# Sparse attention and two expert layers on one core: probabilities transposed as two 64-row halves, and a new order of the vector and scalar work around them

## The chip, the core and the metric

The kernel runs on one core of one Trainium2 chip. The metric is the device time of one execution in microseconds (us): the median of three timed runs. One further execution was recorded by the hardware profiler, and every trace row below is of that one. Engine names are those of the profile: PE (matmul) and PEld (the loads of its stationary operand), DVE (vector), ACT (scalar), POOL (GpSimd), SP (issues most DMAs).

## The reference, cut to what matters

```python
def _attn_ref(q, k, v, n_sink, window):          # q, k, v: (2, 8, 768, 64)
    scores = np.matmul(q, k.transpose(0, 1, 3, 2)) / np.sqrt(D)
    keep = is_sink | in_window                   # key < 4, or 0 <= query - key < 128
    scores = np.where(keep, scores, -1e9)
    a = np.exp(scores - np.max(scores, axis=-1, keepdims=True))
    a = a / (np.sum(a, axis=-1, keepdims=True) + 1e-09)
    return np.matmul(a, v)
...
x = attention output as (1536 tokens, 512)
h = relu(x @ w_in);  x = (h * h) @ w_out         # 512 -> 2048 -> 512
h = x @ w_in2;       out = (h * tanh(softplus(h))) @ w_out2
```

## The kernel before, in words

The attention comes first and the two expert layers follow it on the same engines. In the expert layers every matmul is done three times, on a high and a low part of each operand ("hi" and "lo": hi is the value rounded to a matmul format by ACT, lo is what DVE gets by subtracting hi from the value).

The attention is cut into 12 tiles, one for each of the 2 batch entries and 6 blocks of 128 queries, and each tile into 4 **pairs** of heads, so there are 48 pairs. A written-out loop runs over **slots** `n`, one per pair; in slot `n` several pairs are at work at different stages (`at[d]` is pair `n + d`). The program is emitted under a manual schedule, so each engine runs its instructions in the order in which the loop emits them. The stages of a pair, with the lines of the kernel before:

- `prep` (L302, L314, L320): PE transposes the q or k of a whole tile (4 transposes), ACT rounds it to hi, DVE subtracts for lo. One q and one k per tile, in the even slots.
- `emit_s` (L356): scores, for pair `n + 4`. Each head has 64 rows of contraction, so the two heads of the pair sit in two 64-row halves of the PE array ("64*128" in the trace): six matmuls in three twos, over 128, 256 or 272 key columns. The scores go to two PSUM banks; four banks rotate, so the scores of pair `n + 4` need the banks of pair `n + 2`, and those come free when its exponentials are done.
- `emit_max` (L367): DVE masks the scores in place and takes the row maximum, one instruction for each head (e = 0, 1).
- `emit_exp` (L379): ACT takes the exponentials of pair `n + 3` into `pr`, with row sums.
- `emit_rs` (L390, L391) and `emit_norm` (L399): in even slots, for two pairs, DVE adds up and inverts the sums (`rs`) and POOL multiplies `pr` by them, one instruction per pair. In the last pair of a tile that has separate sink columns (query blocks 2 to 5) POOL also copies those columns to `psg` (`emit_sink`).
- `emit_t` (L407, L408): in even slots PE transposes the probabilities of two pairs, 128 queries x 128 keys each, by a matmul with an identity ("128*128"): 4 transposes per pair (2 in query block 0). `evac_t` (L415) copies each pair's result from PSUM, on DVE for j = 0 of the four, on ACT otherwise.
- `emit_av` (L428): in odd slots the products with v for two pairs, two heads side by side in 64 array columns ("128*64"), each matmul recorded as two. Tiles with sink columns add `emit_sink_t` (L449, one transpose), `evac_sink` (L455, DVE) and `emit_sink_mm` (L464, 16 records).
- `emit_x` (L477) and `split_x` (L483): when a tile's output is complete, in the next slot with n % 4 = 2, ACT rounds it to `xh` and DVE subtracts for `xl`. There is one PSUM buffer for a tile's output, so the next tile's first products wait for `xl`.

Four conversions of expert weights (`Conv`: L131, L137, L141, L147, L162, L166) are laid into fixed slots of the same loop.

So an even slot has, on PE: scores (64*128), 4 transposes of q or k and 8 of probabilities (128*128). An odd slot has: scores (64*128), 16 records of products with v (128*64), and once per sink tile another 16.

Of the kernel before, what the change touches and what calls it, by code (L numbers as in the profile page):

```python
# [9 lines left out]
F32 = mybir.dt.float32  # L10
# [7 lines left out]
P = 128  # L18
# [10 lines left out]
def kernel(  # L29
# [13 lines left out]
    nc = tc.nc  # L43
    B, H, S, D = q.shape
# [4 lines left out]
    NPAIR = H // 2  # L49
# [292 lines left out]
    pair_no = {p: m for m, p in enumerate(pairs)}  # L342

    def sum_at(b, i, j):
        g, s = divmod(pair_no[b, i, j] + 1, 2)
        return sums[g % len(sums)], s
    st = {}
    pr = {}
# [49 lines left out]
        x = pr[b, i][:, 2 * j : 2 * j + 2, 0:w]  # L398
        nc.gpsimd.tensor_tensor(out=x, in0=x, in1=rs.to_broadcast([P, 2, w]), op=ALU.mult)  # L399

    def emit_t(b, i, j):
        _, _, _, op, oc, _ = geom(i)
        pt = ps_p.tile([P, 2, 2, P], F32, tag="pt", name="pt")
        for e in range(2):
            h = 2 * j + e
            if op is not None:
                nc.tensor.transpose(pt[:, 0, e, :], pr[b, i][:, h, op : op + P], ident)  # L407
            nc.tensor.transpose(pt[:, 1, e, :], pr[b, i][:, h, oc : oc + P], ident)  # L408
        st["pt", b, i, j] = pt

    def evac_t(b, i, j):
        pt = st.pop(("pt", b, i, j))
        pts = apool.tile([P, 2, 2, P], F32, tag="pts", name="pts", bufs=3)
        c = slice(0 if i else 1, 2)
        (nc.vector.tensor_copy if j in EV else nc.scalar.copy)(pts[:, c], pt[:, c])  # L415
        st["pts", b, i, j] = pts

    av = {}

    def emit_av(b, i, j):  # L420
        _, _, _, op, _, os_ = geom(i)
        if j == 0:
            av[b, i] = ps_a.tile([P, NPAIR, P], F32, tag="av", name="av")
        pts = st.pop(("pts", b, i, j))
        blocks = [(1, i)] if op is None else [(0, i - 1), (1, i)]
        for m, (c, kb) in enumerate(blocks):
            for e in range(2):
                nc.tensor.matmul(  # L428
                    av[b, i][e * D : (e + 1) * D, j, :], lhsT=vn[b, kb][:, 2 * j + e, :],
                    rhs=pts[:, c, e, :], start=(j == 0 and m == 0),  # L430
                    stop=(j == NPAIR - 1 and m == len(blocks) - 1 and os_ is None),
                    skip_group_check=True,
                )
# [9 lines left out]
    def emit_sink_t(b, i, free):  # L443
        if geom(i)[5] is None:
            return
        g = st.pop("sink")

        pt = free[0][:, 512 - P :] if free else ps_p.tile([P, P], F32, tag="pt", name="trs")
        nc.tensor.transpose(pt, g.rearrange("p h s -> p (h s)"), ident)  # L449
        st["trs"] = pt  # L450

# [42 lines left out]
    with tc.manual_schedule():  # L494
        load_limits()
        nc.scalar.preload_act_table_set("natural_log_exp_and_others")
        load_tile(0, "qk", halves=2)
        load_tile(1, "qk")
        load_tile(2, "kq")
        load_tile(0, "v")  # L500
        load_tile(3, "kq")
        positions()
        load_tile(1, "v")
        load_vsink(0)
        load_tile(2, "v")
        load_tile(3, "v")
        warm = apool.tile([P, P], F32, name="warm")
        nc.vector.memset(warm, 0.0)
        nc.vector.memset(one, 1.0)
        nc.gpsimd.memset(two, 2.0)  # L510
        for x in sums:
            nc.vector.memset(x, 1e-9)
        idle = ps_a.tile([P, P + 2], F32, tag="av", name="idle")

        def keep_warm(times):
            for _ in range(times):
                nc.tensor.matmul(idle[:, 0:P], lhsT=warm, rhs=warm, start=True, stop=True)  # L517

        keep_warm(WARM[0])
        limits(idle[:, P : P + 2])  # L520
        first_mask()
        prep(0, "q", 0)
        place_prep()
        keep_warm(WARM[1])
        prep(0, "k", 0)
        place_prep()
        keep_warm(WARM[2])
        emit_s(*pairs[0])
        emit_max(*pairs[0], 0)
        emit_max(*pairs[0], 1)  # L530
        prep(0, "q", 1)
        place_prep()
        prep(0, "k", 1)
        place_prep()
        emit_s(*pairs[1])
        emit_max(*pairs[1], 0)
        emit_max(*pairs[1], 1)
        second_mask()
        window_masks()
        emit_exp(*pairs[0])  # L540
        for n in range(-3, NPR + 4):
            at = {d: pairs[n + d] for d in range(-3, 5) if 0 <= n + d < NPR}
            last = {d for d in at if at[d][2] == NPAIR - 1}
            t, j = divmod(n, NPAIR)
            if 4 in at and n > -3:
                emit_s(*at[4])
            if 3 in at and n > -3:
                emit_exp(*at[3])
            if n % 2 == 0:
                group = [at[d] for d in (1, 2) if d in at]  # L550
                if group:
                    emit_rs(group)
                for p in group:
                    emit_norm(*p)
                    if p[2] == NPAIR - 1:
                        emit_sink(*p[:2])
            if -3 in last:
                emit_x(*at[-3][:2])
            if 4 in at and n > -3:
                emit_max(*at[4], 0)  # L560
                emit_max(*at[4], 1)
            split_x()


            if n % 2 == 0:
                if n >= 0:
                    prep(t + 2, "kq"[j // 2])
                for d in (-1, 0):
                    if d in at:
                        emit_t(*at[d])  # L570
                if -1 in last:
                    emit_sink_t(*at[-1][:2], st["s", *at[4]][0] if 4 in at else None)
            else:
                for d in (-3, -2):
                    if d in at:
                        emit_av(*at[d])
                if -2 in last:
                    emit_sink_mm(*at[-2][:2])
            if -1 in at:
                evac_t(*at[-1])  # L580
            if n in (-3, -2):
                prep(1, "qk"[n + 3])
            place_prep()
            evac_sink()
            if n >= 0 and j == NPAIR - 1:
                load_tile(t + 4, "q", halves=1 + (t + 5 == len(tiles)))
                load_tile(t + 4, "k")
                load_tile(t + 4, "v")
            if n == -1 or (n >= 0 and t < len(tiles) - 1 and (t % NB, j) == (NB - 1, 2)):
                sink_keys()  # L590
            if n < 0:
                keep_warm(WARM[3])
            if n == 1:
                fast_flag()
                load_vsink(1)
            if n in (5, 13):
                spread_vsink(n // 8)
            for m, x in enumerate(blocks):
                step = CONV_STEPS.get(n - CONV_AT[0] - CONV_AT[1] * m)
                if step:  # L600
                    getattr(x, step)()
# [424 lines left out]
```

## Time and profile before

| | us |
|---|---|
| median of three runs | 633.4 (633.07 to 634.25) |
| profiled execution, its own time | 634.14 |
| its span, first to last instruction | 632.4 |
| last matmul of the attention, about | 106.2 |
| PE busy over the span | 624.2 |

Read it as two programs, one after the other: the attention up to 106.2 us, and the expert layers. Busy time of PE is modelled by the profile from pipelined matmuls; how far apart the starts of loads and matmuls stand tells more. In what follows a cycle is two slots (an even and an odd one), and a tile is two cycles.

### The profile page before, as it was taken

How to read it: one execution, taken by the hardware profiler on the slowest of the kernel's cores; microseconds unless marked ns; L12 is line 12 of the kernel's file. 1: busy time of each engine (PE TensorE's matmuls, PEld its weight loads, DVE VectorE, ACT ScalarE, POOL GpSimd, SP SyncE). 2: the span in 40 equal slices, each digit the busy share in tenths (PEclk: the TensorE clock that was granted, in tenths of full speed). 3: DMA queues.
4: the chain of work that ended last, by engine and by line, in shares of the span. 5: the costliest groups of instructions: out<-in, count | busy, mean ns of one | idle time of the engine just before them, and what ended most of it. 6: DMA issues, size and time to landing. Idle time of an engine off the chain costs nothing.

```text
span 632.4 us, 9265 instructions
## 1 busy us (share of the span) xinstructions
PE 624.2 (99%) x3382; PEld 515.9 (82%) x3382; DVE 461.9 (73%) x968; ACT 363.7 (58%) x745; POOL 71.1 (11%) x97
## 2 busy tenths in 40 slices
PE   8999999999999999999999999999999999999996
PEld 7778787888888888888888888888888888888885
DVE  5988983999852011138889869999888888888884
ACT  5988985777744333347777745555454444544442
POOL 4686773000000000000000000000000000000000
PEclk9999999999999999999999999999999999999999
DMA  8644630666630000005666600000010000010001
GB/s 200 148 118 104 164 120 26 195 204 201 199 101 1 2 0 1 0 1 169 197 199 199 192 10 1 0 2 1 1 66 1 1 1 1 1 67 0 2 0 69
DMA packets 61189, 46.83 MB, mean 74 GB/s; under 512 B 38996, under 2 KB 55636, under 8 KB 61140
## 3 DMA queue, kind: packets, MB, share of 16 engines
q1 hardware_dynamic: 60848, 45.82, 25.0%
q8 instruction: 27, 0.44, 0.3%
q10 hardware_dynamic: 292, 0.39, 0.2%
q14 instruction: 22, 0.18, 0.1%
HBM read 43.06 MB, written 3.15 MB: 73 GB/s over the span
## 4 chain that ended last, share of the span: by engine, by line
PE 96%; DVE 2%; ACT 1%; issue 0%; DVEq 0%
PE h L620 41%; PE o L636 41%; PE s L356 4%; PE av L428 3%; PE tr L302 2%; PE pt L408 1%; PE pt L407 1%; PE idle L517 1%; PE av L464 1%; DVE s L367 1%; ACT pr L379 0%; DVE cv_a L147 0%; DVE cv_r L137 0%; ACT kh L314 0%; DVE cv_r L141 0%
## 5 line engine op out<-in xcount | busy, mean ns | idle before, releaser
L620 PE MATMUL h<-xl,wih 128*128 128x512 f32 x384 | 103.2, 390 | 0.0
L620 PE MATMUL h<-xh,wil 128*128 128x512 f32 x384 | 103.0, 390 | 0.0
L620 PE MATMUL h<-xh,wih 128*128 128x512 f32 x384 | 102.6, 389 | 0.0
L694 DVE TENSOR_TENSOR gl<-h,gh 128x512 fp32r<-128x512 f32 x48 | 33.2, 691 | 93.0 <-ACT gh L690 92.9
L620 PEld LDWEIGHTS h<-xl,wih 128*128 128x128 f32 x384 | 72.0, 188 | 15.2 <-issue 0.3
L620 PEld LDWEIGHTS h<-xh,wih 128*128 128x128 f32 x384 | 72.1, 188 | 15.0
L620 PEld LDWEIGHTS h<-xh,wil 128*128 128x128 f32 x384 | 71.9, 188 | 15.0 <-issue 0.2
L710 ACT ACTIVATE e<-t,small 128x512 f32<-128x512 f32 x48 | 34.8, 726 | 70.1 <-DVE t L706 70.1
L636 PE MATMUL o<-gh,wol 128*128 128x512 f32 x192 | 74.7, 389 | 0.0
L636 PE MATMUL o<-gl,woh 128*128 128x512 f32 x192 | 74.7, 389 | 0.0
L636 PE MATMUL o<-gh,woh 128*128 128x512 f32 x192 | 74.7, 389 | 0.0
L688 ACT ACTIVATE h<-h 128x512 f32<-128x512 f32 x48 | 27.9, 582 | 77.5 <-PE h L620 77.4
L636 PE MATMUL o<-wol,gh 128*128 128x512 f32 x176 | 68.5, 389 | 0.0
L636 PE MATMUL o<-woh,gl 128*128 128x512 f32 x176 | 68.5, 389 | 0.0
L636 PE MATMUL o<-woh,gh 128*128 128x512 f32 x176 | 68.5, 389 | 0.0
L726 ACT CAST gh<-t 128x512 fp32r<-128x512 f32 x44 | 27.4, 623 | 46.6 <-PE o L636 42.9
L399 POOL TENSOR_TENSOR pr<-pr,rs 128x544 f32<-128x544 f32 (+2 forms) x48 | 48.4, 1022 | 23.4 <-DVE rs L391 13.3
L147 DVE SCALAR_TENSOR_TENSOR cv_a<-cv_a,cv_r 128x512 int32<-128x512 int32 x64 | 44.4, 694 | 6.1
L379 ACT ACTIVATE pr<-s,nm 128x272 f32<-128x272 f32 (+2 forms) x96 | 44.4, 476 | 5.0 <-DVE nm L367 2.6
L731 DVE TENSOR_TENSOR gl<-t,gh 128x512 fp32r<-128x512 f32 x44 | 30.3, 690 | 19.8 <-ACT gh L726 19.8
L636 PEld LDWEIGHTS o<-gh,wol 128*128 128x128 f32 x192 | 36.1, 188 | 7.5
L636 PEld LDWEIGHTS o<-gl,woh 128*128 128x128 f32 x192 | 36.0, 188 | 7.5
(121 smaller groups left out, 1101.2 us busy)
## 6 DMA issues: line engine op xcount, KB each, us to landing
raw<-in_moe_w_in_dram SPq DMA_DIRECT2D x32, 512.0 KB, 3.8
raw<-in_moe_w_out_dram SPq DMA_DIRECT2D x32, 512.0 KB, 4.0
vn<-in_v_dram SPq DMA_DIRECT2D x12, 256.0 KB, 3.0
kn<-in_k_dram SPq DMA_DIRECT2D x11, 256.0 KB, 3.7
qn<-in_q_dram SPq DMA_DIRECT2D x10, 256.0 KB, 4.1
out_dram<-ob SPq DMA_DIRECT2D x8, 256.0 KB, 2.2
qn<-in_q_dram SPq DMA_DIRECT2D x4, 128.0 KB, 3.0
out_dram<-o SPq DMA_DIRECT2D x2, 256.0 KB, 2.9
```

The costliest lines, as they stand in the source:

```text
L147: nc.vector.scalar_tensor_tensor(out=ai, in0=ai, scalar=3, in1=self.r, op0=ALU.logical_shift_left, op1=ALU.bitwise_or)
L356: nc.tensor.matmul(banks[e][:, 0:w], lhsT=x[b, i][r, j, :], rhs=y[r, j, c0 : c0 + w], start=(m == 0), stop=(m == 2),)
L379: nc.scalar.activation(out=pr[b, i][:, 2 * j + e, 0:w], in_=banks[e][:, 0:w], func=AF.Exp, bias=nm[:, e : e + 1], scale=-1.0, accum_out=sm ...
L399: nc.gpsimd.tensor_tensor(out=x, in0=x, in1=rs.to_broadcast([P, 2, w]), op=ALU.mult)
L428: nc.tensor.matmul(av[b, i][e * D : (e + 1) * D, j, :], lhsT=vn[b, kb][:, 2 * j + e, :], rhs=pts[:, c, e, :], start=(j == 0 and m == 0), s ...
L620: nc.tensor.matmul(ph, lhsT=w[a][:, d, :], rhs=x[:, d, :], start=(m == 0 and d == 0), stop=(m == 2 and d == NDC - 1),)
L636: nc.tensor.matmul(acc[sp][t], lhsT=a, rhs=x, start=(fb == 0 and m == 0), stop=(fb == NFB - 1 and m == 2),)
L688: nc.scalar.activation(out=ph, in_=ph, func=AF.Relu)
L694: nc.vector.tensor_tensor(out=gl, in0=hp.pop(n), in1=f32(gh), op=ALU.subtract)
L710: nc.scalar.activation(out=e, in_=t, func=AF.Ln, bias=two)
L726: nc.scalar.copy(g_tiles(n)[0], et[n][1])
L731: nc.vector.tensor_tensor(out=gl, in0=t, in1=f32(gh), op=ALU.subtract)
```

## The change

- `emit_t` takes two pairs at once, and each 128 x 128 transpose becomes two: rows 0 to 63 and rows 64 to 127 of the queries, each with the 64 x 64 corner of the identity that lies on the same rows, written to a bank of its own (`banks[r]`). 176 transposes become 352 of half the rows and half the output columns. `evac_t` now copies one such bank (both pairs, half of the queries) per slot, r = 0 in the even slot on ACT, r = 1 in the odd slot, on DVE every other time.
- The two pairs transposed in slot n are n and n + 1 (they were n - 1 and n). The row sums of pairs n + 2 and n + 3 are inverted in slot n (they were n + 1 and n + 2), so the exponentials of pair n + 3, in the same slot, come before them.
- `emit_rs` and `emit_norm` stand behind both maxima of the slot. They stood ahead of them.
- `emit_x` (rounding of the output, ACT) stands ahead of the slot's exponentials; `split_x` (DVE) between the two maxima. The sink transpose follows the scores of an odd slot, and its copy stands between the maxima.
- `prep` moves to the odd slots, and k is prepared one tile further ahead.

```diff
     def sum_at(b, i, j):
-        g, s = divmod(pair_no[b, i, j] + 1, 2)
+        g, s = divmod(pair_no[b, i, j], 2)
...
-    def emit_t(b, i, j):
-        _, _, _, op, oc, _ = geom(i)
-        pt = ps_p.tile([P, 2, 2, P], F32, tag="pt", name="pt")
-        for e in range(2):
-            h = 2 * j + e
-            if op is not None:
-                nc.tensor.transpose(pt[:, 0, e, :], pr[b, i][:, h, op : op + P], ident)
-            nc.tensor.transpose(pt[:, 1, e, :], pr[b, i][:, h, oc : oc + P], ident)
-        st["pt", b, i, j] = pt
...
+    def emit_t(group):
+        banks = [ps_p.tile([P, 2, 2, 2, P // 2], F32, tag="pt", name="pt") for _ in range(2)]
+        for s, (b, i, j) in enumerate(group):
+            _, _, _, op, oc, _ = geom(i)
+            for e in range(2):
+                for c, o in enumerate((op, oc)):
+                    if o is None:
+                        continue
+                    for r in range(2):
+                        rows = slice(r * D, (r + 1) * D)
+                        nc.tensor.transpose(
+                            banks[r][:, s, c, e, :], pr[b, i][rows, 2 * j + e, o : o + P], ident[rows, rows]
+                        )
+        pts = apool.tile([P, 2, 2, 2, P], F32, tag="pts", name="pts", bufs=2)
+        for s, p in enumerate(group):
+            st["pts", p] = pts[:, s]
+        st["evac"] = [(group, banks[r], pts[..., r * D : (r + 1) * D], r) for r in range(2)]
+
+    def evac_t(eng=None):
...
+        copy = nc.vector.tensor_copy if r and pair_no[group[0]] % 4 in EV else nc.scalar.copy
...
             if 4 in at and n > -3:
                 emit_s(*at[4])
+            if 0 in last:
+                emit_sink_t(*at[0][:2], st["s", *at[4]][0][1] if 4 in at else None)
+            if -3 in last:
+                emit_x(*at[-3][:2])
             if 3 in at and n > -3:
                 emit_exp(*at[3])
+            if 4 in at and n > -3:
+                emit_max(*at[4], 0)
+            evac_sink()
+            split_x()
+            if 4 in at and n > -3:
+                emit_max(*at[4], 1)
             if n % 2 == 0:
-                group = [at[d] for d in (1, 2) if d in at]
+                group = [at[d] for d in (2, 3) if d in at]
                 if group:
                     emit_rs(group)
                 for p in group:
                     emit_norm(*p)
                     if p[2] == NPAIR - 1:
                         emit_sink(*p[:2])
-            if -3 in last:
-                emit_x(*at[-3][:2])
-            if 4 in at and n > -3:
-                emit_max(*at[4], 0)
-                emit_max(*at[4], 1)
-            split_x()
...
             if n % 2 == 0:
-                if n >= 0:
-                    prep(t + 2, "kq"[j // 2])
-                for d in (-1, 0):
-                    if d in at:
-                        emit_t(*at[d])
-                if -1 in last:
-                    emit_sink_t(*at[-1][:2], st["s", *at[4]][0] if 4 in at else None)
+                if 0 in at:
+                    emit_t([at[0], at[1]])
             else:
+                if n >= -1:
+                    prep(*((t + 3, "k") if j == NPAIR - 1 else (t + 2, "q")))
                 for d in (-3, -2):
                     if d in at:
                         emit_av(*at[d])
                 if -2 in last:
                     emit_sink_mm(*at[-2][:2])
-            if -1 in at:
-                evac_t(*at[-1])
+            evac_t()
...
-            evac_sink()
```

PE's instructions in one even slot before, in the middle of the attention (`tr` is the transposed q or k, `pt` the transposed probabilities; "x2" stands for the two 64-row halves):

```order
L356 MATMUL s<-kh,qh 128x272 x2
L356 MATMUL s<-kh,ql 128x272 x2
L356 MATMUL s<-kl,qh 128x272 x2
L302 MATMUL tr<-ident,qn 128x128 x4
L407 MATMUL pt<-ident,pr 128x128
L408 MATMUL pt<-ident,pr 128x128
L407 MATMUL pt<-ident,pr 128x128
L408 MATMUL pt<-ident,pr 128x128
L407 MATMUL pt<-ident,pr 128x128
L408 MATMUL pt<-ident,pr 128x128
L407 MATMUL pt<-ident,pr 128x128
L408 MATMUL pt<-ident,pr 128x128
```

PE's instructions after, an even slot (the first four rows) and most of the odd slot behind it:

```order
L356 MATMUL s<-kh,qh 128x272 x2
L356 MATMUL s<-kh,ql 128x272 x2
L356 MATMUL s<-kl,qh 128x272 x2
L411 MATMUL pt<-ident,pr 128x64 x16
L356 MATMUL s<-kh,qh 128x272 x2
L356 MATMUL s<-kh,ql 128x272 x2
L356 MATMUL s<-kl,qh 128x272 x2
L462 MATMUL s<-ident,psg 128x128
L302 MATMUL tr<-ident,kn 128x128 x4
L441 MATMUL av<-pts,vn 64x128 x8
```

The 128-row transposes of q or k left the even slot for the odd one, between the scores and the products with v, and the probabilities' transposes, now of 64 columns, stand between two groups of scores.

DVE's instructions in a slot that rounds a tile's output, before (the instruction on `s,nm` is the masked maximum, the one on `nm` alone its readout):

```order
L390 TENSOR_REDUCE rs<-sum_105 128x4
L391 RECIPROCAL rs<-rs 128x4
L367 ISA s,nm<-s,mask_e 128x272
L367 ISA nm 128x1
L367 ISA s,nm<-s,mask_e 128x272
L367 ISA nm 128x1
L483 TENSOR_TENSOR xl_70<-av,xh_67 128x4x128
L320 TENSOR_TENSOR ql<-tr,qh 128x512
```

DVE's instructions in such a slot after:

```order
L367 ISA s,nm<-s,mask_e 128x272
L367 ISA nm 128x1
L496 TENSOR_TENSOR xl_70<-av,xh_67 128x4x128
L367 ISA s,nm<-s,mask_e 128x272
L367 ISA nm 128x1
L390 TENSOR_REDUCE rs<-sum_105 128x4
L391 RECIPROCAL rs<-rs 128x4
```

The inversion of the row sums went from ahead of the two maxima to behind them, and the subtraction of the output came between them.

## Rows read from the trace of the kernel before

**Rows 1.** The page's head: span, and busy time of each engine.

```profile
span 632.4 us, 9265 instructions
...
PE 624.2 (99%) x3382; PEld 515.9 (82%) x3382; DVE 461.9 (73%) x968; ACT 363.7 (58%) x745; POOL 71.1 (11%) x97
```

**Rows 2.** Windows: length, then busy us (x instructions) of PE, PEld, DVE, ACT, POOL.

```profile
18.11:96.39 78.28, 76.77 (x862) 63.52 (x860) 69.89 (x266) 69.80 (x226) 57.74 (x63) 1.00 0.50 129
106.20:632.40 526.20, 521.20 (x2300) 431.34 (x2298) 378.63 (x641) 279.26 (x474) 0.00 (x0) 1.00 0.20 63
...
25.29:32.53 7.24, 7.24 (x82) 5.97 (x80) 6.51 (x27) 7.00 (x23) 4.75 (x6) 1.00 0.41 93
32.53:41.84 9.31, 8.31 (x99) 7.00 (x97) 8.44 (x27) 7.25 (x24) 6.92 (x8) 1.00 0.58 153
41.84:50.08 8.24, 8.24 (x100) 6.97 (x98) 6.88 (x28) 7.34 (x23) 7.51 (x8) 1.00 0.44 100
```

**Rows 3.** Chain that ended last, 25 to 33 us: start, us, what.

```profile
25.36 0.57 PE s L356 x6
...
26.52 0.11 PE pt L407
...
27.39 0.57 PE s L356 x6
27.96 1.02 PE av L428 x16
```

**Rows 4.** Timeline, PE's weight loads: start, us, line, rows*columns, count, idle before.

```profile
100.30 0.14 PEld L407 LDWEIGHTS pt<-ident,pr 128*128 128x128 f32 x1 [0.17 <-issue]
100.36 0.14 PEld L408 LDWEIGHTS pt<-ident,pr 128*128 128x128 f32 x1
100.47 0.14 PEld L407 LDWEIGHTS pt<-ident,pr 128*128 128x128 f32 x1
...
46.45 0.19 PEld L356 LDWEIGHTS s<-kh,qh 64*128 64x128 f32 x2 [0.17 <-ACT pr L379]
46.56 0.19 PEld L356 LDWEIGHTS s<-kh,ql 64*128 64x128 f32 x2
46.68 0.19 PEld L356 LDWEIGHTS s<-kl,qh 64*128 64x128 f32 x2
```

**Rows 5.** Timeline of DVE, ACT and POOL, 45 to 49 us.

```profile
45.65 0.49 ACT L379 ACTIVATE pr<-s,nm 128x272 f32<-128x272 f32 x1
...
46.02 0.15 DVE L390 TENSOR_REDUCE rs<-sum 128x4 f32<-128x8 f32 x1
...
46.47 1.09 POOL L399 TENSOR_TENSOR pr<-pr,rs 128x544 f32<-128x544 f32 x1 [0.41 <-DVE rs L391]
...
46.58 0.60 ACT L477 CAST xh<-av 128x512 fp32r<-128x512 f32 x1
...
47.13 0.45 DVE L367 CUSTOM_DVE_ANT_0 s<-s,mask_o 128x272 f32<-128x272 f32 x1 [0.74 <-PE s L356]
...
47.49 0.48 DVE L367 CUSTOM_DVE_ANT_0 s<-s,mask_o 128x272 f32<-128x272 f32 x1
...
47.89 0.69 DVE L483 TENSOR_TENSOR xl<-av,xh 128x512 fp32r<-128x512 f32 x1
```

**Rows 6.** Timeline of PE at the attention's end, 98 to 107 us.

```profile
98.18 0.73 PE L620 MATMUL h<-xh,wil 128*128 128x512 f32 x2
...
101.15 0.71 PE L620 MATMUL h<-xh,wil 128*128 128x512 f32 x2
101.70 0.40 PE L620 MATMUL h<-xl,wih 128*128 128x512 f32 x1
102.03 1.09 PE L428 MATMUL av<-pts,vn 128*64 128x128 f32 x16
...
104.33 0.50 PE L620 MATMUL h<-xl,wih 128*128 128x512 f32 x1
...
106.22 0.73 PE L620 MATMUL h<-xl,wih 128*128 128x512 f32 x2
```

More of the change, by code (lines that the diff above doesn't have):

```diff
@@ L399, in emit_norm @@
         nc.gpsimd.tensor_tensor(out=x, in0=x, in1=rs.to_broadcast([P, 2, w]), op=ALU.mult)
-    def emit_t(b, i, j):
-        _, _, _, op, oc, _ = geom(i)
-        pt = ps_p.tile([P, 2, 2, P], F32, tag="pt", name="pt")
-        for e in range(2):
-            h = 2 * j + e
-            if op is not None:
-                nc.tensor.transpose(pt[:, 0, e, :], pr[b, i][:, h, op : op + P], ident)
-            nc.tensor.transpose(pt[:, 1, e, :], pr[b, i][:, h, oc : oc + P], ident)
-        st["pt", b, i, j] = pt
[L411 to L416, printed above, removed]
+    def emit_t(group):
[16 more added lines that the diff above has]
+    def evac_t(eng=None):
+        if not st.get("evac"):
+            return
+        group, x, y, r = st["evac"].pop(0)
+        copy = nc.vector.tensor_copy if r and pair_no[group[0]] % 4 in EV else nc.scalar.copy
+        c0 = [0 if i else 1 for _, i, _ in group]
+        if len(set(c0)) == 1:
+            copy(y[:, : len(group), c0[0] :], x[:, : len(group), c0[0] :])
+        else:
+            for s, c in enumerate(c0):
+                copy(y[:, s, c:], x[:, s, c:])
     av = {}
@@ L423, in emit_av @@
             av[b, i] = ps_a.tile([P, NPAIR, P], F32, tag="av", name="av")
-        pts = st.pop(("pts", b, i, j))
+        pts = st.pop(("pts", (b, i, j)))
         blocks = [(1, i)] if op is None else [(0, i - 1), (1, i)]
@@ L446, in emit_sink_t @@
         g = st.pop("sink")
-        pt = free[0][:, 512 - P :] if free else ps_p.tile([P, P], F32, tag="pt", name="trs")
+        pt = free[:, 512 - P :] if free is not None else ps_p.tile([P, P], F32, tag="pt", name="trs")
         nc.tensor.transpose(pt, g.rearrange("p h s -> p (h s)"), ident)
```

## The prediction

> **What bounds the kernel now.** First the page's head: PE is busy in 624.2 of 632.4 us [rows 1], so time can only be won where PE is freed, and PE's busy time has to be looked at stage by stage. Then the windows: from 106.2 us on PE is busy in 521.2 of 526.2 us, and the change touches nothing there [rows 2]. Everything happens in the attention. Between 18.11 and 96.39 us, ten tiles, DVE is busy for 69.89 and ACT for 69.80 of 78.28 us [rows 2]: 89% each, so two engines stand close behind PE. Then the chain that ended last: in a steady cycle it is PE alone, from 25.36 us to 27.96 + 1.02 = 28.98 us, 3.62 us with no wait in it [rows 3]. A tile is two such cycles, 7.24 us, which is the length of the window 25.29 to 32.53; a tile with sink products has 0.87 us more on PE and takes 8.24 us in the window 41.84 to 50.08 [rows 2]. So PE sets the pace now, and the others have 0.2 to 1.4 us of air per tile.
>
> **What PE gains.** The eight transposes of a cycle start at 26.52 us and end at 27.39 us, 0.87 us, 0.109 us each [rows 3]. What is in those 0.109 us decides the first term. In the timeline of the weight loads, the first load of a group starts at 100.30 us, the second at 100.36, the third at 100.47 [rows 4]. The second load follows the first at once, after 0.06 us, so one load takes 0.06 us; the third waits 0.11 us, and what it waits for can only be the first matmul of 128 columns, at about 0.107 us. A half transpose moves 64 columns, 0.054 us, and loads 128 columns, 0.06 us. Two halves lie on different 64-row halves of the array, and the scores show how such two behave: both loads of a two are recorded as one piece, and the twos follow each other by 0.12 us (46.56 to 46.68) with 272 columns [rows 4]. So I take 0.058 us per two halves. The trace has no half transpose; the bounds are 0.054 us (two halves beside each other, the matmul alone) and 0.218 us (two transposes one after the other, each at the old 0.109). I take the low end since the operation is a transpose and both halves are placed as the scores' are. Eight twos per cycle: 0.46 us for 0.87, a gain of 0.41.
>
> The Trainium skill ("TensorE: Matmul & The Clock Gate", LDWEIGHTS) says that a load takes its columns over 1.2 per ns, whatever the rows: 107 ns for 128 columns. By that rule a half transpose would load as long as a whole one, a two would stay at 0.107 us, and the 0.41 us would be nothing. The 0.06 us between the first two loads speaks against it here; it is a rival below.
>
> The second gain is a change of the array's shape. Where PE goes from one shape (64*128, 128*128, 128*64) to another, the load stands idle for 0.17 us at 46.45 and 100.30 us [rows 4]. A cycle has four such changes now: into the transposes, back, into the products with v, back. Afterwards probabilities are transposed in the scores' shape, so an even slot has none, and an odd slot three (64*128 to 128*128 for q or k, to 128*64, back). One less per cycle, 0.17 us. PE's cycle becomes 3.62 - 0.41 - 0.17 = 3.04 us: 0.84 in the even slot (three twos of scores at 0.125, and 0.46) and 2.20 in the odd one. A tile would take PE 6.1 us, or 6.95 with sink products.
>
> **What takes its place.** PE at 6.1 us a tile would be below ACT and DVE, at 69.8 / 10 = 6.98 us a tile. But before that another chain closes, through the moved row sums. I walk it in the slot that rounds the output, times from its first score load (46.45 us in the rows). Now: rounding at 0.13, maxima at 0.68 and 1.04, subtraction at 1.44, while the inversion had begun at 46.02, ahead of all this, and POOL's multiplication followed 0.45 us after it began, for 1.09 us [rows 5]. After: rounding 0.13 to 0.73, first maximum 0.68 to 1.04, subtraction (0.69) to 1.73, second maximum (0.40) to 2.13, inversion and hand-over (0.45) to 2.58, two multiplications of 1.09 to 4.76. The exponentials that the sums wait for stand behind the rounding on ACT; two of them took from 45.65 to 46.58, 0.93 us [rows 5], so they end at 1.66 and are not late. The transposes of the second of these pairs, in the next even slot, can't start before 4.8; PE alone would have been there at 3.04 + 0.38 + 0.23 = 3.65. So PE waits there about 1.1 us per tile. Behind them come 0.23 us of transposes, then the odd slot, 2.20, with sink products 0.87 more, and the next tile's rounding can begin only after that. The tile is 4.8 + 0.23 + 2.20 = 7.23 us, or 8.10 with sink products, against 7.24 and 8.24 now [rows 2]. The chain through DVE and POOL gives back nearly all that PE gains.
>
> The other moves I cost at nothing inside a tile. The scores of the pair after the rounding must wait for banks until the exponentials end at 1.66 instead of starting at 0.84, but that idle time lies inside the same 4.8. The transposes of q and k keep their 0.44 us in a slot that has no other transposes; q and k are needed four slots later at the earliest. The evacuations copy as many columns as before, one per slot, and each has the rest of the cycle. The sink copy between the maxima delays the second by 0.3 us in an odd slot, where DVE waits for nothing of POOL. If these covers fail, each costs at most its own length once per tile, 0.3 to 0.6 us. The four weight conversions cost 9.31 - 8.24 = 1.07 us in the tile that shows one [rows 2]; I take the same afterwards, with bounds of 0 and twice that for each of four.
>
> **The end of the attention.** From 102.03 to 106.22 us, 4.19 us, PE does 16 records of products, the last transposes, 8 records, an expert matmul, 8 records and 16 sink records [rows 6]. Afterwards the last two groups of products stand behind each other: 1.02 + 0.87 + 0.87 + 0.17 = 2.9 us, 1.3 less. The last two groups of transposes are shorter by 0.41 each, 0.8, with no scores behind them that need more. Against this, six expert matmuls fill gaps before 106.22 now [rows 6], and the new order has two there; four come later, at 521.2 / 2300 = 0.23 us each, 0.9. Sum: -1.2 us.
>
> **Sum.** Six tiles with sink products at -0.14 make -0.8, four without at -0.01 nothing, the end -1.2: -2.0 us. The profiled execution took 634.14 us, so 632.1; it lay 0.74 above the median of 633.4, so the median becomes **631.4 us**.
>
> **Rivals.**
> - *The chain is shorter than I walk it.* If PE reaches its slots with DVE ahead, the multiplications start earlier, and ACT and DVE bound at 6.98 us a tile. All of it would be 78.28 - 69.9 = 8.4 us; I take half, with the end 5.4 us: 628.0. For it: both are busy now for only 89%. Against it: the order on DVE is fixed, and 4.76 is made of rows.
> - *A two costs 0.109 us after all* (the load bounds it). Then the second pair's transposes take 0.44 for 0.23, tiles 7.44 and 8.31: 4 x 0.20 + 6 x 0.07 = +1.2, and the end wins 0.4: +0.8, 634.2. That is the case where the transposes win nothing.
> - *The sums come later still* (the other side). Now DVE may fall behind by a microsecond without PE noticing, since the sums are ahead of the maxima. Afterwards every delay of DVE or ACT in an even slot reaches POOL and then PE. A conversion's operations, or exponentials that wait for the rounding longer than I reckon, give it. At 0.2 us more per tile the gain is gone; at 0.5 it is +5.0 - 2.0: 636.4. For it speaks DVE with 8.44 busy us in the tile with a conversion [rows 2].
> - *The two halves go one after the other.* Eight twos at 0.218 are 1.74 for 0.87 us; with the change of shape saved, +0.7 per cycle on some 22 cycles: +15, 649.
>
> **Chances.** Forecast 45 (32 faster, 11 same, 2 slower, for the errors of the walk), shorter chain 13 (faster), load-bound 15 (2, 9, 4), later sums 22 (3, 4, 15), one after the other 5 (slower). 0.2%, 1.3 us, is about what a measurement of this kernel can tell from no change. So faster 0.50, same 0.24, slower 0.26. Cut off the serial case and the far ends of the two neighbours: 627.8 to 635.4; the forecast's own range is 629.5 to 633.
>
> **What would show it.** Starts of `pt` loads in twos 0.06 us apart, in one row group each, and no idle load between scores and transposes: right on PE. Their start waiting for POOL L399 about once per tile, and DVE's inversion starting 2.1 us behind the slot's first score load: right on the chain. Tiles under 7 us would show the first rival, rows of `pt` at 0.11 us per two the second, the inversion at 2.5 us or later the third. I am wrong if the attention ends (last sink products) much before 104 or after 106.5 us.

## The result and the profile after

Six runs of the changed kernel took 638.17 us in the median (636.77 to 639.47), six of the kernel before beside them 633.80 (632.93 to 634.47): a ratio of 1.0071, interval [1.0058, 1.0084]. The change costs 4.4 us, where 2.0 less were forecast. The profiled execution took 637.74 us.

The page's head of the kernel after, as in [rows 1]:

```profile
span 636.0 us, 9619 instructions
...
PE 622.5 (98%) x3558; PEld 513.6 (81%) x3558; DVE 464.2 (73%) x966; ACT 363.8 (57%) x745; POOL 71.4 (11%) x97
```

PE has 1.7 us less to do and the span is 3.6 longer. Windows of the kernel after, columns as in [rows 2]; the first three are three tiles, from a tile's first scores to the next one's, then the stretch from tile 2's first scores to those of the last pair, and the expert layers:

```profile
25.93:33.39 7.46, 7.15 (x100) 5.69 (x98) 6.55 (x26) 6.97 (x23) 4.78 (x6) 1.00 0.43 98
33.39:41.91 8.52, 7.85 (x116) 6.57 (x114) 8.11 (x26) 6.54 (x22) 6.94 (x8) 1.00 0.56 154
41.91:51.25 9.34, 8.30 (x115) 6.62 (x113) 7.27 (x29) 8.16 (x25) 7.10 (x8) 1.00 0.41 93
17.95:96.36 78.41, 72.01 (x990) 58.05 (x989) 68.40 (x249) 67.23 (x218) 56.89 (x62) 1.00 0.48 124
109.20:636.00 526.80, 522.30 (x2308) 431.99 (x2304) 378.72 (x641) 279.45 (x474) 0.00 (x0) 1.00 0.20 63
```

PE is busy 72.01 of 78.41 us in the attention's tiles, where it was 76.77 of 78.28 [rows 2]: it was freed and now stands. To see where the time is lost, four points of each trace, in us of the span (the starts of tile 2's first scores, of the last pair's scores and of the last sink product, and the end), and the stretches between them:

| kernel | tile 2 | last pair | sinks end | end | tiles | end of attention | rest |
|---|---|---|---|---|---|---|---|
| before | 18.11 | 94.39 | 106.02 | 632.42 | 76.28 | 11.63 | 526.40 |
| after | 17.95 | 96.36 | 109.20 | 636.00 | 78.41 | 12.84 | 526.80 |

So +2.1 in the tiles, +1.2 at the attention's end, +0.4 behind it; the start gives back 0.2. Forecast were -0.8 in the tiles and -1.2 for the end and behind it together. The points are of one execution each: tile 2 begins at 17.95 us here, and at 17.36 and 18.42 in two kernels of the experiments (`conv`, `nca`) that differ from this one only later, so half a microsecond either way is chance.

**What was right.** Weight loads of the kernel after, between two groups of scores, columns as in [rows 4]:

```profile
26.16 0.19 PEld L356 LDWEIGHTS s<-kl,qh 64*128 64x128 f32 x2
26.29 0.38 PEld L411 LDWEIGHTS pt<-ident,pr 64*128 64x128 f32 x8
26.96 0.32 PEld L411 LDWEIGHTS pt<-ident,pr 64*128 64x128 f32 x8 [0.29 <-POOL pr L399]
27.20 0.20 PEld L356 LDWEIGHTS s<-kh,qh 64*128 64x128 f32 x2
```

Eight loads, four twos, take 0.24 us from 26.96 to 27.20, 0.06 us per two as I took it, and no load stands idle for a change of shape. The one idle time here is a wait for POOL. The chain that ended last, as in [rows 3], shows why:

```profile
21.79 0.48 ACT qh L314
22.29 0.69 DVE ql L320
22.98 0.36 DVE s L367
...
24.77 2.16 POOL pr L399 x2
...
26.97 0.50 PE pt L411 x8
...
28.00 1.05 ACT pr L379 x4
29.05 0.48 ACT qh L314
29.52 0.58 ACT xh L490
30.11 0.50 ACT pr L379 x3
...
31.10 0.64 PE s L356 x5
...
35.21 0.77 DVE cv_r L137
36.00 1.23 DVE cv_r L141
...
39.18 0.60 DVE cv_a L147
```

It was PE alone; now it goes through POOL's multiplications into the transposes, and through ACT's exponentials and rounding into the scores; further down it goes through the steps of a weight conversion on DVE (L137 and L141, sign and low word; L147, the joining). The slot that rounds the output, which I walked from its first score load (here 29.39 us): DVE and POOL in the timeline of the kernel after.

```profile
31.48 0.16 DVE L390 TENSOR_REDUCE rs<-sum 128x4 f32<-128x8 f32 x1
31.68 0.18 DVE L391 RECIPROCAL rs<-rs 128x4 f32<-128x4 f32 x1
32.03 2.15 POOL L399 TENSOR_TENSOR pr<-pr,rs 128x544 f32<-128x544 f32 x2 [1.64 <-ACT pr L379]
```

The inversion starts at 2.09 (walked: 2.13), POOL ends at 4.79 (walked: 4.76).

**What was not.** The next such slot begins at 37.59 us and meets a weight conversion. Timeline of DVE and POOL around it:

```profile
34.15 1.54 POOL L131 TENSOR_SCALAR cv_a<-raw 128x512 f32<-128x512 f32 x1
...
35.12 0.84 DVE L137 TENSOR_SCALAR cv_r<-raw 128x512 int32<-128x512 int32 x1
...
35.66 2.48 POOL L399 TENSOR_TENSOR pr<-pr,rs 128x544 f32<-128x544 f32 x2
...
36.00 1.23 DVE L141 TENSOR_SCALAR cv_r<-raw 128x512 uint16<-128x512 uint32 x1
...
37.13 0.45 DVE L367 CUSTOM_DVE_ANT_0 s<-s,mask_e 128x272 f32<-128x272 f32 x1
...
39.09 0.69 DVE L147 SCALAR_TENSOR_TENSOR cv_a<-cv_a,cv_r 128x512 int32<-128x512 int32 x1
39.69 0.45 DVE L367 CUSTOM_DVE_ANT_0 s<-s,mask_e 128x272 f32<-128x272 f32 x1
...
41.01 0.16 DVE L390 TENSOR_REDUCE rs<-sum 128x4 f32<-128x8 f32 x1
...
41.74 2.15 POOL L399 TENSOR_TENSOR pr<-pr,rs 128x544 f32<-128x544 f32 x2 [1.45 <-DVE rs L391]
```

L137 begins beside POOL's L131 and takes 0.84 us, L141 beside a multiplication and takes 1.23. The maxima of the slot before are late, then the evacuation, the subtraction for q's low part, L147; the slot's own first maximum comes 2.1 us behind its scores (0.68 in the walk), the inversion 3.4 (2.13), and POOL starts 4.15 behind them (2.58). Between two rounding slots lie 9.66 us here and 8.20 in the sink tile ahead of it. Grouped by line over 18 to 100 us, the kernel after, then the same group of the kernel before (busy, mean ns):

```profile
L141 DVE TENSOR_SCALAR cv_r<-raw 128x512 uint16<-128x512 uint32 x5 | 5.2, 1047 | 0.1
```
```profile
L141 DVE TENSOR_SCALAR cv_r<-raw 128x512 uint16<-128x512 uint32 x5 | 2.6, 528 | 0.1
```

The kernel before had the same in one of its conversions. Its timeline of DVE and POOL, the first conversion and the second:

```profile
33.85 2.14 POOL L399 TENSOR_TENSOR pr<-pr,rs 128x544 f32<-128x544 f32 x2
...
35.23 1.05 DVE L137 TENSOR_SCALAR cv_r<-raw 128x512 int32<-128x512 int32 x1
...
35.94 0.85 POOL L273 TENSOR_SCALAR_AFFINE_SELECT vs<-vc 128x512 f32<-128x512 f32 x1
36.31 0.80 DVE L141 TENSOR_SCALAR cv_r<-raw 128x512 uint16<-128x512 uint32 x1
...
53.78 0.42 DVE L137 TENSOR_SCALAR cv_r<-raw 128x512 int32<-128x512 int32 x1
54.23 0.46 DVE L141 TENSOR_SCALAR cv_r<-raw 128x512 uint16<-128x512 uint32 x1
```

The waits of the kernel after, 0 to 112 us (us in total, times, longest):

```profile
ACT xh L490 <- PE av L477: 10.6, 8, 2.8
...
PEld pt L411 <- POOL pr L399: 6.3, 13, 0.7
PEld s L356 <- ACT pr L379: 5.2, 21, 0.5
...
PE pt L411 <- POOL pr L399: 4.1, 11, 0.5
```

**The end of the attention.** Two conversions fall together there, the last of the four and the first that the expert layers make for themselves (L137 and L141 at 90.34 and 90.98 us, and again at 92.96 and 95.32), and DVE is late with everything. Windows of the kernel after:

```profile
97.00:98.00 1.00, 0.26 (x2) 0.07 (x1) 1.00 (x4) 0.62 (x3) 0.00 (x0) 1.00 0.55 86
98.00:99.00 1.00, 0.74 (x8) 0.77 (x10) 0.96 (x6) 0.62 (x4) 0.06 (x1) 0.52 0.94 369
99.00:104.00 5.00, 4.72 (x50) 4.09 (x48) 1.85 (x8) 2.67 (x9) 4.31 (x5) 0.50 0.04 14
```

PE stands for most of 97 to 98 us, with DVE busy throughout; from 98 us on the granted clock is 0.50, the 1.2 GHz level, until about 104.9. PE's rows there:

```profile
98.26 1.98 PE L441 MATMUL av<-pts,vn 128*64 128x128 f32 x16 [1.00 <-DVE xl L496]
...
103.52 1.70 PE L477 MATMUL av<-pst,vs 128*64 128x128 f32 x16
```

The wait is for the subtraction of the output; the 16 records behind it take 1.98 us instead of 1.09. In the kernel before the clock is 1.00 throughout this stretch.

### The profile page after: what moved, and what is told of

It is laid out like the page before. It is cut to its first block, busy times and chain, and to the rows that moved or that the text cites. A ratio compares the mean times of both kernels' runs of the same rounds, so it can differ in the third digit from the quotient of the medians.

```text
span 636.0 us, 9619 instructions
## 1 busy us (share of the span) xinstructions
PE 622.5 (98%) x3558; PEld 513.6 (81%) x3558; DVE 464.2 (73%) x966; ACT 363.8 (57%) x745; POOL 71.4 (11%) x97
## 4 chain that ended last, share of the span: by engine, by line
PE 89%; DVE 4%; POOL 3%; ACT 2%; issue 1%; POOLq 0%; DVEq 0%; ACTq 0%
PE h L631 41%; PE o L647 41%; POOL pr L399 3%; PE av L441 2%; PE s L356 2%; ACT pr L379 1%; DVE s L367 1%; PE tr L302 1%; PE pt L411 1%; PE av L477 1%; PE idle L530 1%; DVE ql L320 0%; DVE cv_r L141 0%; ACT xh L490 0%; DVE xl L496 0%
## 5 line engine op out<-in xcount | busy, mean ns | idle before, releaser
L147 DVE SCALAR_TENSOR_TENSOR cv_a<-cv_a,cv_r 128x512 int32<-128x512 int32 x64 | 44.2, 691 | 6.2
```

What stands on the lines that cost most here:

```text
L147: nc.vector.scalar_tensor_tensor(out=ai, in0=ai, scalar=3, in1=self.r, op0=ALU.logical_shift_left, op1=ALU.bitwise_or)
```

## The experiments

Each was timed beside runs of the kernel before (633.2 to 633.5 us in the median). Diffs are against the kernel after, unless another is named.

**1. Whole transposes.** Are the halves themselves the cost?

```diff
...
-                    for r in range(2):
-                        rows = slice(r * D, (r + 1) * D)
-                        nc.tensor.transpose(
-                            banks[r][:, s, c, e, :], pr[b, i][rows, 2 * j + e, o : o + P], ident[rows, rows]
-                        )
+                    nc.tensor.transpose(banks[s][:, c, e, :], pr[b, i][:, 2 * j + e, o : o + P], ident)
...
```

> The changed kernel with whole 128-row transposes again; order and all else stay. Theory C (the row sums reach GpSimd late, PE waits for the multiplied probabilities): PE waits about 9 us in the attention, and the 0.4 us per cycle that the whole transposes cost more on PE partly fall into later stages; the time grows by 2 to 5 us over the changed kernel, to 640 to 643. Theory H (the halves themselves are what costs): the time falls back to 633 to 635. Theory X (rounding ahead of the exponentials): as C.

639.02 us, 1.0088 [1.0075, 1.0101]. With whole transposes the new order is no faster (0.8 us slower, with intervals that overlap): the halves are not what costs. How much they win here this does not tell: the five runs with whole transposes have a mean granted clock of 0.997 to 0.999, five of the six of the kernel after 0.992 to 0.995, and the sixth, at 1.0, took 636.77 us, over 2 us less than with whole transposes.

**2. The order on ACT and DVE.** First both moves undone in their sense (rounding behind the exponentials, subtraction behind the inversion), then the subtraction alone.

```diff
-            if -3 in last:
-                emit_x(*at[-3][:2])
             if 3 in at and n > -3:
                 emit_exp(*at[3])
+            if -3 in last:
+                emit_x(*at[-3][:2])
...
-            split_x()
...
                         emit_sink(*p[:2])
+            split_x()
```

> The changed kernel with the output's rounding behind the exponentials again and its subtraction behind both maxima and the inversion of the row sums. Theory X (it is the rounding's place that costs): back to within 1 us of before, 633 to 635. Theory C: the inversion comes 0.7 us earlier in one slot per tile, so of the 9 us of waits for the multiplied probabilities some 3 go: 635 to 636.5. Theory H: no change, 638.

> The kernel after with the subtraction of the output behind both maxima and the inversion on DVE; ACT's rounding stays ahead of the exponentials. It takes apart the 2.7 us that both moves together gave. If the subtraction's 0.69 us ahead of the inversion is what makes POOL late (theory DVE order): 635.5 to 636, all or most of the gain. If the rounding ahead of the exponentials is (theory ACT order: the exponentials hold the banks of the next scores): 637.5 to 638, nothing.

Both: 635.46 us, 1.0029 [1.0018, 1.0040]. The subtraction alone: 636.78 us, 1.0058 [1.0045, 1.0071]. So the subtraction's place is worth about half of the 2.7 us (1.4, with intervals that overlap), the rounding's the rest (1.3, with intervals that do not); neither theory of a single culprit holds.

**3. More room between multiplication and transposes.** Transposes, products with v, sinks and rounding come one slot later (and two, with `- 2`). In the one-slot form the rounding and its subtraction thereby fall into slots that invert nothing, and q and k are prepared in the even slots again; the two-slot form keeps both as in the kernel after.

```diff
+            lt = {d: pairs[n - 1 + d] for d in range(-3, 2) if 0 <= n - 1 + d < NPR}
...
-            if n % 2 == 0:
-                if 0 in at:
-                    emit_t([at[0], at[1]])
+            if n % 2 == 1:
+                if 0 in lt:
+                    emit_t([lt[0], lt[1]])
...
-                        emit_av(*at[d])
+                        emit_av(*lt[d])
```

> The changed kernel with transposes, products with v and all behind them one slot later against scores, exponentials and sums; the order on DVE and ACT within a slot stays, the rounding one slot later too. Theory C: GpSimd gets about 1.9 us more, the waits of PE for it go from 9 us to under 2; PE then is held by ACT and DVE at 7.0 us per tile, and the time falls below before: 628 to 632. Theory X: rounding still stands ahead of the exponentials, 637 to 639. Theory H: 638.

> The same two slots later. Theory C: waits of PE for GpSimd are gone altogether, but the attention's end comes up to 2 us later since the last pairs go through two more slots: 629 to 634. Theory X: 637 to 640. Theory H: 638 to 640.

> One slot later and the output's rounding behind the exponentials together. Theory C with X (late sums and late exponentials are two separate costs, 3.6 and 2.7 us when undone alone): 631.5 to 633, level with before or below. If both undo the same loss: 634 to 635.

One slot: 634.58 us, 1.0022 [1.0012, 1.0031]; two: 635.23, 1.0030 [1.0019, 1.0041]; one slot with the order of experiment 2: 633.57, 1.0007 [0.9998, 1.0016]. With one slot or two the trace has no wait of `pt` for POOL any more; with one, 3.6 of the 4.4 us are back, and with two, where nothing else was moved, 2.9. That shows the chain as the way in which the time is lost, but not yet what makes it late. By its four points (16.98, 95.01, 105.31 and 632.32 us) the one-slot form wins little of this in the tiles (78.04 for 78.41) and most at the attention's end (10.30 for 12.84), where its clock stayed at 1.00. Of its eleven runs three at a mean granted clock of 1.0 took 633.27 to 634.05 us and three at 0.995 took 635.20 to 635.79: a run with a stretch at 1.2 GHz is nearly 2 us longer. How much of this is the clock's, and how much belongs to what made it fall, the runs do not part.

**4. Keeping PE busy at the end** by four dummy matmuls in each of two slots.

```diff
+                if n in (41, 43):
+                    for _ in range(4):
+                        nc.tensor.matmul(
+                            st["s", *at[4]][0][0][:, 384:512], lhsT=warm, rhs=warm, start=True, stop=True
+                        )
```

> The changed kernel with four matmuls that nothing reads ahead of the products with v in slots 41 and 43, where PE waits for the output's subtraction. Theory K (the clock granted to PE falls to half at 98 us because PE stands, and that costs 1 to 2.5 us): the granted clock stays 1.0 to the end of the attention and the time falls to 636 to 637. If the clock costs nothing: 638 to 639.

639.40 us, 1.0095 [1.0081, 1.0109], with the granted clock at 0.71 from 95 to 100 us. The clock fell earlier than without them (at 94.4 instead of 98.0 us); this tells nothing of the clock's price.

**5. The conversions' first part moved off POOL's multiplications.** Sign and low word (`mid_r`) ahead of an inversion in an even slot, the joining (`mid_or`) still one slot later; on the kernel after, and on that of one slot later with the order of experiment 2. Their old places are taken out of `CONV_STEPS`, as in experiment 6; so too in experiments 7 and 8.

```diff
+    MIDS = (12, 22, 30, 40)
...
+            if n in MIDS:
+                blocks[MIDS.index(n)].mid_r()
...
+            if n - 1 in MIDS:
+                blocks[MIDS.index(n - 1)].mid_or()
```

> The changed kernel with the first step of the four weight conversions (two operations on the vector engine) put into even slots ahead of the inversion, the second step one slot behind. Theory D (the moved multiplications on GpSimd now run beside these operations and stretch them, L141 from 0.47 to 1.24 us, about 3 us in all, in tiles that the vector engine holds): L141 falls to about 0.5 us, and the time by 1.5 to 3 us, to 635 to 636.5, though the inversion comes 0.9 us later in four slots. Theory C alone: those four inversions come later, so 638 to 640.

> One slot later, rounding behind the exponentials and the conversions' first step ahead of the inversion. Theories C, X and D together: 629.5 to 632, faster than before. If D is nothing: as the kernel with the first two, within 0.5 us.

637.82 us, 1.0078 [1.0063, 1.0093], and 636.01, 1.0043 [1.0030, 1.0057]: no gain over the kernel after, and 2.4 us lost against the same kernel without the move (633.57), where a gain had been expected. The groups of the first by line, 18 to 100 us:

```profile
L147 DVE SCALAR_TENSOR_TENSOR cv_a<-cv_a,cv_r 128x512 int32<-128x512 int32 x5 | 5.5, 1125 | 0.0
L141 DVE TENSOR_SCALAR cv_r<-raw 128x512 uint16<-128x512 uint32 x5 | 2.5, 519 | 0.1
```

L141 is back at 519 ns, but now the joining runs beside POOL, and L147 takes 1,125 ns. The stretch had only changed its place, and this did not decide.

**6. Conversions without their steps on DVE,** in the kernel after (`nca`) and in the kernel before (`ncb`).

```diff
-    CONV_STEPS = {0: "load", 5: "head_pool", 7: "mid_r", 8: "mid_or", 11: "high", 12: "low_pool"}
+    CONV_STEPS = {0: "load", 5: "head_pool", 11: "high", 12: "low_pool"}
```

> The kernel after without the two middle steps of the four weight conversions on DVE in the attention (sign and low word, L137 and L141, and the joining, L147); the first expert layer's weights are then wrong in value, nothing else is left out. Theory conversions (they run under POOL's multiplications now, 1.0 us instead of 0.5 each, and this is most of the loss): the gap to the kernel before with the same steps left out falls from 4.4 us to 1.5 or less, so about 630 to 631. Theory chain (inversion, multiplication and transposes in one line, conversions or not): the gap stays at 3.5 us or more, so 632 to 634. DVE alone, without any overlap, is freed of 4 x 1.56 = 6.2 us.

> The kernel before without the same steps. A tile with a conversion was 1.07 us longer than one without in the profile, four of them: 629.0 if the steps stand on the path there, 633 if the time in these tiles has another reason. It is the other half of the comparison with the kernel after without the steps.

633.12 us (0.9994 [0.9985, 1.0003]) and 632.35 (0.9982 [0.9973, 0.9990]). The steps cost 638.17 - 633.12 = 5.0 us after, and 633.51 - 632.35 = 1.2 before; without them 0.8 us of the 4.4 are left. The gap fell as the theory of the conversions had it; the time did not (630 to 631 expected), since the steps cost 1.2 us before and not four times 1.07. One thing else changes: without the steps the expert layers' own first conversion comes earlier in both kernels (its L137 at 84.40 instead of 92.96 us after, at 81.60 instead of 89.10 before), so a part of the 5.0 us may be that one's. A window of `nca` over the stretch in which the clock fell:

```profile
95.00:100.00 5.00, 4.23 (x68) 3.52 (x68) 2.52 (x12) 3.72 (x12) 3.39 (x4) 1.00 0.00 0
```

DVE has half of it free and the clock stays up. And a window of `ncb`, the tile that holds the first conversion, 9.31 us long with the steps [rows 2]:

```profile
32.01:40.25 8.24, 8.24 (x99) 6.97 (x98) 6.62 (x26) 6.99 (x23) 7.17 (x8) 1.00 0.51 141
```

**7. Conversions where POOL stands.** Both parts in even slots ahead of the inversion, the joining two slots later: on the kernel of experiment 3's last form (`d1xe`) and on the kernel after (`ceven`).

```diff
+            if n in MIDS:
+                blocks[MIDS.index(n)].mid_r()
+            if n - 2 in MIDS:
+                blocks[MIDS.index(n - 2)].mid_or()
             if n % 2 == 0:
                 group = [at[d] for d in (2, 3) if d in at]
```

> The transposes, products and rounding one slot later, the rounding behind the exponentials, the subtraction behind the inversion, and the middle steps of the conversions in even slots, ahead of the inversion, where POOL stands: sign and low word in slots 12, 22, 30 and 40, the joining two slots later. Theory conversions: L137, L141 and L147 fall to 0.42, 0.46 and 0.68 us, and the time to 631.5 to 633, under the 633.6 of the same kernel without the move. Theory chain: the 1.0 us and 0.7 us ahead of the inversion make POOL as late as the stretch made DVE: 633.5 to 636.

> The kernel after, with both middle parts of each conversion in even slots, ahead of the inversion, where POOL stands: sign and low word in slots 12, 22, 30 and 40, the joining two slots later. Theory overlap (what the conversions cost after is that they run at POOL's pace beside its multiplications): L137, L141 and L147 go to 0.42, 0.46 and 0.68 us and the time to 633.5 to 635. Theory place (any 0.7 to 0.9 us on DVE ahead of an inversion makes POOL and the transposes late, stretched or not): no gain, 637 to 639.

633.81 us, 1.0009 [1.0000, 1.0019], and 635.98, 1.0043 [1.0030, 1.0056]. `d1xe` wins nothing over the 633.57 us without the move, and as its L141 still takes 704 ns in the mean, it tells little of the overlap. In `ceven` L137 and L141 take 430 and 516 ns in the mean, L147 still 898. It wins 2.2 us of the 5.0, so the overlap is a part. That the mere place of 0.7 to 0.9 us ahead of an inversion is another, and the end of the attention, where two conversions still meet, a third, is argued from the rows; the shares were not measured.

**8. Conversions spread out and done before the end.** Experiment 3's last form, a conversion every eight slots.

```diff
-    CONV_AT = (5, 9)
+    CONV_AT = (5, 8)
+    CONV_STEPS = {0: "load", 5: "head_pool", 12: "high", 13: "low_pool"}
...
+    MIDS = (12, 20, 28, 36)
...
+            if n in MIDS:
+                blocks[MIDS.index(n)].mid_r()
+            if n - 4 in MIDS:
+                blocks[MIDS.index(n - 4)].mid_or()
```

> The kernel with transposes, products and rounding one slot later, with the conversions every eight slots instead of nine: sign and low word in slots 12, 20, 28 and 36, the joining four slots later, both ahead of the inversion and in slots without a rounding; the last one is done before the end of the attention begins. Theory overlap: 631.5 to 633, faster than the kernel before, with the granted clock at 1.0 between 90 and 100 us. Theory place: 633.5 to 635.

> The same kernel (one slot later, conversions as in the kernel after) without the two middle steps of the conversions on DVE; the first expert layer's weights are wrong in value. It shows what the halves and the one slot more are worth when DVE has room: if the conversions are all that hold it, 2 to 3 us less than the kernel before without the steps (632.35), so 629.5 to 630.5; if ACT's and DVE's own busy time bounds the tiles, 631.5 to 632.5.

629.76 us, 0.9945 [0.9933, 0.9958]: 3.5 us under the kernel before, below what either theory expected, and the version to keep. Its joining takes 0.69 us in four of five cases (0.72 in the other), but the overlap is not gone: its L141 takes 699 ns in the mean. Against `d1xe`, from which it differs in the conversions' slots alone (points 17.46, 91.82, 103.95 and 630.81 us), it is 1.0 us shorter in the tiles and 2.1 at the attention's end. Its clock holds where that of the kernel after fell:

```profile
95.00:100.00 5.00, 4.96 (x85) 4.28 (x83) 1.48 (x3) 2.17 (x4) 1.96 (x3) 1.00 0.02 5
```

Without the steps (`d1nc`) the kernel of one slot later took 630.50 us, 0.9958 [0.9944, 0.9972], 1.9 less than the kernel before without them: so much the halves, the new order and the slot more are worth together when no conversion is in the way. What the halves alone are worth there, no run with whole transposes in that order shows. It is not below `d1x8`. Its clock fell in the profiled run (0.50 from 88 to 91 us), but two runs at a mean clock of 1.0 took 630.19 and 630.29 us as well; `d1x8` also has the conversions' loads and their steps on POOL and ACT in other slots, and what gives the last 0.5 us is open.

## Why the prediction was wrong

The same four points, in us, for the kernels that decide it:

| kernel | tiles | end of attention | rest |
|---|---|---|---|
| before, without the steps | 75.32 | 11.27 | 525.95 |
| after, without the steps | 75.92 | 10.30 | 526.81 |
| one slot later, conversions every eight slots | 73.34 | 10.06 | 526.98 |

- *What PE gains* was right: 0.06 us per two halves, and one change of shape less. The rule of the Trainium skill that I set against it ("TensorE: Matmul & The Clock Gate", LDWEIGHTS: 107 ns for a load of 128 columns) does not agree with these rows: a two of such loads follows the one before it after 0.06 us.
- *The chain that takes its place* was right: to 0.04 us in the slot that I walked. Without conversions a sink tile takes 8.20 us from rounding to rounding (8.10 forecast; 8.23 before), one without sinks 7.71 (7.23 forecast; 7.40 before). The 0.48 us above the forecast are in the chain: the subtraction for q's low part (ql, from 22.29 us), which `prep` brought into the odd slot, ends in the rounding slot, ahead of its first maximum. That slot begins at 21.69 us; its first maximum comes 1.21 us later (walked: 0.68), and POOL ends at 5.23 (walked: 4.76). So "the other moves I cost at nothing" was wrong for this one: the reason given asks when PE needs q and k, and not when DVE has to work on them. That the slot walked came out to 0.04 us is in part luck, for the walk leaves ql out there too, where it began 0.17 us behind the scores and was out of the way in time. In all the tiles came out +0.6 us where -0.8 was forecast.
- *The end of the attention* is half right for the kernel without the steps: 11.27 to 10.30 us, 1.0 won where I had counted 2.1 from the rows, and 0.9 more behind it for the four matmuls that come later, as forecast. The sum is -0.1, not -1.2; which of the counted rows fell short was not followed up.
- *The step that failed* is "The four weight conversions cost 9.31 - 8.24 = 1.07 us in the tile that shows one [rows 2]; I take the same afterwards". They cost 5.0 us instead of 1.2, which is most of the 6.4 us between forecast and result. Four times 1.07 is near the cost afterwards; it was not the cost before. There the tile of the first conversion is 9.31 us long with the steps and 8.24 without (experiment 6), that of the second 7.88 both ways, that of the third 7.61 and 7.24: the tile I read was the one whose L137 and L141 ran beside POOL. By the points of the traces, about half of the difference between 5.0 and 1.2 lies in the tiles (+2.5 after, +1.0 before) and half at the attention's end and behind it (+2.5 after, +0.8 before), where two conversions meet. I had looked at what stands on DVE ahead of the inversion, and not at what POOL would now run beside: after the change POOL's multiplications begin where the conversions' steps stand, and L141 takes 1,047 ns in the mean there instead of 528. How much of the cost is this stretch, how much the steps' place and how much their meeting at the end stays open. The delay goes down the chain that I had named, as the third rival says ("a conversion's operations ... give it"), and at the end PE stands and the clock falls. The attention ends (last sink products) at 109.2 us, past the 106.5 that the prediction named as a sign of being wrong.
- That the fall of the clock is caused by PE's standing was not shown by itself (experiment 4 does not show it). The runs at a full clock show that it is not the whole: the one of the kernel after took 636.77 us, still 3 us more than before.

The rival of later sums had 636.4 us. It was the right one in kind; that it is also the nearest in size is partly luck, since it put 5.0 us into the tiles, where the steps cost 2.5, and nothing at the end. I gave it 0.22, since I took the longest tile as a sign of DVE's load and did not ask how long its operations would take in another place.

## What to carry to other kernels

When a change moves work on one engine, list which instructions of the others will run beside it afterwards, and look in the trace for rows of these in both situations: in the trace of the kernel before, L137 stands with 0.42 and with 1.05 us and L141 with 0.46 and 0.80, if one looks. A chain with no slack turns such rows into time; two slots more between producer and consumer took out 2.9 of 4.4 us without a faster instruction. Before a faster engine can pay, the occasional work (here the conversions) needs places of its own, away from the stage's end: with the slot more, other slots for the conversions won nothing as long as two of them met at the end (633.81 us), and 3.8 us when they did not (633.57 to 629.76).

## What the runs showed of the hardware

- DVE's operations on SBUF alone take longer when they begin while POOL works (on its multiplication of 128 x 544, or on L131 or L273): L141 0.46 to 1.24 us, L137 0.42 to 0.84 and more, L147 0.68 to 1.58 (`ceven`). L141 from 36.00 us ends 0.32 us after the multiplication that ran when it began (36.91), and so does the one from 72.81 (73.73). L137 from 72.38 us, which began before POOL did (72.64), took 0.40. The masked maximum (scores in PSUM, mask in SBUF) that ran from 37.13 us while POOL multiplied took 0.45, as ever. The Trainium skill ("SBUF — State Buffer", Who interferes with whom) says that DVE and GpSimd share a port pair under an exclusive lock, and that DVE instructions with at most one SBUF input, outside the two-port modes, don't contend. The rows agree for L147, which reads two inputs from SBUF, and for the masked maximum. L137 and L141 read one, so by that rule they would contend only in a two-port mode, and no run here shows in which mode they ran. A step that has to wait for what is left of one multiplication of 1.07 us (2.15 / 2) would be up to 1.1 us longer, an estimate, and L141 is 0.8 longer.
- While PE stood for 1.0 us, waiting for DVE, the granted clock fell to the 1.2 GHz level; it stayed there for 6.8 us (98.0 to 104.9), and 16 records took 1.98 us instead of 1.09. Standing is not all of it: in `d1x8` PE was busy for 3.97 of 5 us from 90 to 95 us, and the clock stayed at 1.00. What decides was not settled.
